# Attention, two-expert routing and an ELU layer on one core: rooms of 312 rows, a third conversion buffer with later stores, and ELU as a maximum

## The chip, the cores and the metric

The kernel is one program for one core of a Trainium2 chip. The metric is device time in microseconds (us). Five engines of the core matter here: TensorE (PE in the rows; its weight loads are PEld), VectorE (DVE), ScalarE (ACT), GpSimd (POOL) and SyncE (SP), which issues nearly all transfers (DMAs) and executes them strictly in its own order.

## What is computed

Three stages follow one another. Attention over 2 batches and 8 heads gives a matrix x of 1152 tokens by 512. A layer of 8 experts follows, of which each token uses two. A dense layer with an ELU ends the program. The reference, cut to the parts that the change touches:

```python
# experts: every token goes to the two experts with the largest noisy logits
for e in range(8):
    for k in range(2):
        mask = top2[:, k] == e
        h = np.maximum(x[mask] @ w1[e], 0.0)              # w1[e]: 512 x 1024
        out[mask] += top2_w[mask, k, None] * (h @ w2[e])  # w2[e]: 1024 x 512
# dense layer, w_in 512 x 2048 and w_out 2048 x 512, both float64
h = x @ w_in
g = np.where(h > 0.0, h, np.exp(np.minimum(h, 0.0)) - 1.0)
return g @ w_out
```

Counted with the reference on its own inputs, the eight experts receive 293, 306, 271, 255, 298, 284, 290 and 307 rows, and expert 0 receives 156 from the first batch and 137 from the second.

## The kernel before

**Rooms.** Each expert's rows are scattered into a room of fixed size in a DRAM tensor `xs`. Experts 1 to 7 have rooms of `CAP` = 336 rows; expert 0 has two rooms of `HC` = 168 rows, one per batch, together `E0` = 336. Rows beyond a room would be handled by a fallback (`overflow`), entered only if a count on the device is above zero. A whole room is computed, filled or not.

**Products.** Every float32 matrix product is made of three products of split operands (high and low halves in the `fp32r` type). ScalarE writes the high half, VectorE or GpSimd subtract it to get the low half. For an expert, layer 1 (L731) is 8 groups of 12 matmuls whose moving operand is a row block of `CAP` columns; layer 2 (`l2t`, L741) is 4 groups of 24 matmuls with `CAP` columns. Expert 0 has its own first layer (`First.l1`, L844, 168 columns), and expert 7 has a layer 2 in another form (`l2`, L759, 512 columns), in which the room's rows are the stationary operand.

**Conversions.** `w_in` and `w_out` arrive as float64. While the experts run, 32 pieces of them are converted with bit operations (`plan_convert`): a load of 512 KB into one of two `raw64` buffers (L697), four VectorE steps (L701 to L704), two GpSimd steps in place on the tile `cvm` (L707, L708), and a store of 256 KB to a DRAM tensor `wf` (L710), from which the dense layer later loads its weights.

**Order.** The order of work on all engines is written out: each step is given a time on an imaginary line (`ln.at`), and steps are emitted in the order of these times. An expert takes D = 29.7 units of the line; the conversion i stands at 16.5 + 5.99 i, its load 3 units before, its GpSimd steps 2 units behind, its store 6 units behind:

```python
m=s['m']=cv.tile([128,512],FT,name="cvm",bufs=2)
ln.at(t-3,load); ln.at(t,bits); ln.at(t+2,small); ln.at(t+6,store)
```

The time line sets only the order. When an instruction starts is decided by its engine's queue and by semaphores, so an instruction that waits holds up all that stand behind it on its engine. On SP a store that waits for GpSimd holds back the loads behind it.

**ELU.** The dense layer runs in three chunks of 384 tokens. For each of 16 groups of a chunk, PE makes `a` in PSUM (L972, 12 matmuls of 384 columns), `act` turns it into the halves g2h and g2l, and two groups later PE uses them in 9 matmuls of 512 columns (`outs`, L991). `act` has six steps, alternating between the engines:

```python
nc.scalar.activation(r,a[:,0:384],AF.Relu)
nc.vector.tensor_scalar(m,a[:,0:384],0.0,None,op0=OP.min)
nc.scalar.activation(m,m,AF.Exp)
nc.vector.scalar_tensor_tensor(r,m,-1.0,r,op0=OP.add,op1=OP.add)
```

then g2h on ScalarE (L981) and g2l on VectorE (L982). In the first chunk ScalarE and GpSimd also split the last weights (L670, L674).

## Time and profile before

| | before |
|---|---|
| median of the runs | 825.7 us (825.38, 825.7, 841.67) |
| profiled execution, its own time | 819.85 us |
| its span | 818.1 us, granted TensorE clock 0.99 of full speed |
| PE busy | 786.0 us, 96% |
| VectorE / ScalarE / GpSimd busy | 585.6 / 482.4 / 328.2 us |
| data moved | 119.82 MB, mean 146 GB/s |

The profile shows one execution, with times from the start of its span. The stages are read best by stretches: attention and the first layer of expert 0 up to about 336 us, the experts from there to about 607 us, the dense layer behind it. A busy PE is not a PE at its peak, since matmuls overlap; what a matmul costs is read from the distance between the starts of two matmuls in a row.

### The profile page before, as it was taken

To read this page: it belongs to the slowest core of one execution; us is meant where nothing else is said; L and a number is where in the kernel's file an instruction comes from. 1 tells how busy PE (TensorE), PEld (TensorE's weight loads), DVE (VectorE), ACT (ScalarE), POOL (GpSimd) and SP (SyncE) were. 2 spreads that over 40 slices of the span, in tenths; PEclk is the share of its full clock that TensorE was granted. 3 is DMA by queue.
4 is the path that set the end of the run, shared out by engine and by line. 5 is a ranking of instruction groups with operands and counts; after the bars stand their busy time and mean duration, and the time that the engine had idled before them with its cause. 6 is when DMAs were issued, how large, how long until landed. Compare 5 with 4: busy or idle time off the path is not lost.

```text
span 818.1 us, 13530 instructions
## 1 busy us (share of the span) xinstructions
PE 786.0 (96%) x4891; PEld 721.4 (88%) x4891; DVE 585.6 (72%) x1182; ACT 482.4 (59%) x1109; POOL 328.2 (40%) x303
## 2 busy tenths in 40 slices
PE   7999999999999999989999999999999899999997
PEld 5898989998888889979899999999887799999996
DVE  6888898898999876586968778687555644454443
ACT  5988888989888864434444445445345434334432
POOL 4634051431510765266666677666516602000000
PEclk8999999999999999989999999999999999999999
DMA  8029465131002245559688898986743203001001
GB/s 251 2 93 274 136 230 178 40 128 57 29 30 105 91 138 198 187 179 309 228 287 262 274 306 279 295 275 218 263 125 115 64 14 104 1 14 38 1 1 40
DMA packets 50984, 119.82 MB, mean 146 GB/s; under 512 B 7574, under 2 KB 8598, under 8 KB 50914
## 3 DMA queue, kind: packets, MB, share of 16 engines
q1 hardware_dynamic: 47922, 109.35, 40.6%
q0 software_dynamic: 2912, 9.44, 3.6%
q8 instruction: 40, 0.66, 0.3%
q14 instruction: 30, 0.25, 0.1%
q10 hardware_dynamic: 80, 0.13, 0.0%
HBM read 82.89 MB, written 36.01 MB: 145 GB/s over the span
## 4 chain that ended last, share of the span: by engine, by line
PE 30%; DMA 11%; DVE 9%; ACT 3%; issue 2%; POOL 2%; SPq 0%; DVEq 0%; POOLq 0%; ACTq 0%
PE o L991 11%; PE a L972 10%; PE oe L741 5%; DMA raw<-in_moe_w_in_dram 5%; DMA raw<-in_moe_w_dram 3%; PE ae L731 3%; DVE wl L674 2%; DMA raw<-in_moe_w_out_dram 2%; ACT wh L670 1%; DVE cvt L703 1%; DVE cvm L701 1%; DVE r L979 1%; DMA raw<-wf 1%; POOL cvm L708 1%; DVE cvt L704 1%
## 5 line engine op out<-in xcount | busy, mean ns | idle before, releaser
L293 ACT ACTIVATE p<-sp,m 128x384 f32<-128x384 f32 x216 | 125.1, 585 | 13.2 <-DVE m L285 13.0
L282 DVE TENSOR_REDUCE m<-sp 128x1 f32<-128x384 f32 x216 | 115.4, 550 | 20.6 <-PE sp L277 18.8
L674 POOL TENSOR_TENSOR wl<-raw,wh 128x1024 fp32r<-128x1024 f32 x32 | 80.8, 2530 | 59.3 <-ACT wh L670 59.2
L670 ACT ACTIVATE wh<-raw 128x1024 fp32r<-128x1024 f32 x76 | 79.8, 1057 | 37.9 <-DMA raw<-in_moe_w_dram 36.7
L305 DVE TENSOR_TENSOR pl<-t_p,ph 128x512 fp32r<-128x512 f32 x144 | 96.8, 683 | 6.0 <-ACT ph L302 4.2
L302 ACT ACTIVATE ph<-t_p 128x512 fp32r<-128x512 f32 x144 | 86.2, 603 | 16.7 <-PE t_p L299 11.3
L299 PE MATMUL t_p<-ident,p 128*128 128x128 f32 x576 | 83.3, 274 | 1.2 <-ACT xt L363 0.7
L277 PE MATMUL sp<-khl,qh 128*128 128x384 f32 x192 | 75.6, 394 | 4.2 <-ACT p L293 3.7
L299 PEld LDWEIGHTS t_p<-ident,p 128*128 128x128 f32 x576 | 67.9, 140 | 9.9 <-ACT xt L363 0.9
L707 POOL TENSOR_SCALAR cvm<-cvm 128x512 f32<-128x512 f32 x32 | 51.3, 1602 | 38.9 <-DVE cvm L701 38.9
L277 PE MATMUL sp<-khl,ql 128*128 128x384 f32 x192 | 65.7, 342 | 0.0
L674 DVE TENSOR_TENSOR wl<-raw,wh 128x1024 fp32r<-128x1024 f32 x44 | 63.4, 1453 | 2.6 <-ACT wh L670 2.6
L310 PE MATMUL o<-ph,vhl 128*128 128x512 f32 x144 | 63.8, 443 | 0.0
L991 PE MATMUL o<-wh,g2h 128*128 128x512 f32 x144 | 57.1, 396 | 3.9 <-ACT g2h L981 3.9
L234 POOL TENSOR_SCALAR kr<-kraw 128x576 fp32r<-128x576 f32 x14 | 9.5, 678 | 126.2 <-PE t_k L241 126.2
L311 PE MATMUL o<-pl,vhl 128*128 128x512 f32 x144 | 57.3, 398 | 1.0 <-DVE pl L305 1.0
L991 PE MATMUL o<-wh,g2l 128*128 128x512 f32 x144 | 56.8, 394 | 0.0
L991 PE MATMUL o<-wl,g2h 128*128 128x512 f32 x144 | 56.3, 391 | 0.0
L977 DVE TENSOR_SCALAR m<-a 128x384 f32<-128x384 f32 x48 | 26.7, 556 | 40.9 <-ACT r L976 40.2
L708 POOL TENSOR_TENSOR cvm<-cvm,cvt 128x512 f32<-128x512 f32 x32 | 48.0, 1501 | 17.3 <-DVE cvt L704 17.3
L979 DVE SCALAR_TENSOR_TENSOR r<-m,r 128x384 f32<-128x384 f32 x48 | 34.3, 714 | 28.4 <-ACT m L978 27.8
L701 DVE TENSOR_SCALAR cvm<-raw 128x512 int32<-128x512 int32 x32 | 26.9, 839 | 34.8 <-DMA raw<-in_moe_w_in_dram 19.9
(269 smaller groups left out, 1987.4 us busy)
## 6 DMA issues: line engine op xcount, KB each, us to landing
raw<-in_moe_w_dram SPq DMA_DIRECT2D x60, 512.0 KB, 7.1
raw<-in_moe_w_in_dram SPq DMA_DIRECT2D x16, 512.0 KB, 7.7
wf<-cvm SPq DMA_DIRECT2D x32, 256.0 KB, 2.8
raw<-in_moe_w_out_dram SPq DMA_DIRECT2D x16, 512.0 KB, 8.3
raw<-wf SPq DMA_DIRECT2D x16, 512.0 KB, 4.6
xs<-zrow SPq DMA_DIRECT2D x3, 1792.0 KB, 15.1
xs<-zrow SPq DMA_DIRECT2D x2, 2560.0 KB, 22.9
xe<-xs SPq DMA_DIRECT2D x7, 672.0 KB, 9.4
```

What stands on the lines that cost most here:

```text
L277: nc.tensor.matmul(sp[:,g,0:384],w,kh[:,h,384*(g0+g):384*(g0+g)+384],start=i==0,stop=i==len(ops)-1)
L282: nc.vector.tensor_reduce(m[:,x:x+1],s['s',j,x][:,:,0:384],axis=AX.XY,op=OP.max,negate=True)
L293: nc.scalar.activation(s['p',j][:,384*g0:384*(g0+nb)].rearrange("p (g n) -> p g n",g=nb),s.pop(('s',j,x))[:,:,0:384],AF.Exp,bias=m[:,3:4], ...
L299: nc.tensor.transpose(t[:,jj*128:jj*128+128],s['p',4*h+jj][:,kt*128:kt*128+128],ident)
L302: nc.scalar.activation(ph,s['tp',h,kt],AF.Copy)
L305: nc.vector.tensor_tensor(pl,s.pop(('tp',h,kt)),s['ph',h,kt].bitcast(FT),op=OP.subtract)
L310: nc.tensor.matmul(s['o',h],w,s.pop(('ph',h,kt)),start=kt==0,stop=False)
L311: nc.tensor.matmul(s['o',h],w,s.pop(('pl',h,kt)),start=False,stop=kt==8)
L670: s.tc.nc.scalar.activation(w[0][:,p['i']*p['n']:(p['i']+1)*p['n']],p['r'],AF.Copy)
L674: e.tensor_tensor(w[1][:,sl],p['r'],w[0][:,sl].bitcast(FT),op=OP.subtract)
L972: nc.tensor.matmul(a[:,0:384],wv[:,c,fs],xv[:,c],start=n==0,stop=n==11); n+=1
L991: nc.tensor.matmul(O[i],gv[:,ts],wv[:,f%8],start=f==0 and n==0,stop=f==15 and n==2)
```

## The change

Three edits. The rooms of experts 1 to 7 shrink to 312 rows, and expert 0 keeps its 336. The conversions follow one another every 5.7 units of the line (5.99 before), their stores stand 8 units behind (6 before), and `cvm` has three buffers (two before). In `act` the first step becomes Relu(-a) on ScalarE, the exponential is taken of its negative on ScalarE, and one VectorE step makes max(exp - 1, a), reading `a` from PSUM; the step L977 goes away. Since 104 rows (a third of a room) and 84 rows are no multiples of 16, loads and stores of rooms are issued in two strips (96 and 8 rows, 80 and 4 rows). The diff, cut to what has a part in the time:

```diff
+def strips(m):
+    return [(a,b) for a,b in ((0,m//16*16),(m//16*16,m)) if b>a]
-HC=168; E0=2*HC; CAP=336; C3=CAP//3; OVR=102; OV0=E0+7*CAP; OVN=1632; NROW=OV0+OVN+128; NDUMP=20*128
+HC=168; E0=2*HC; CAP=312; C3=CAP//3; EM=max(E0,CAP); OVR=105; OV0=E0+7*CAP; OVN=1680; NROW=OV0+112*17; NDUMP=20*128
...
-        f=s['f']=cv.tile([128,512],I32,name="cvt",bufs=2); m=s['m']=cv.tile([128,512],FT,name="cvm",bufs=2)
+        f=s['f']=cv.tile([128,512],I32,name="cvt",bufs=2); m=s['m']=cv.tile([128,512],FT,name="cvm",bufs=3)
...
-    ln.at(t-3,load); ln.at(t,bits); ln.at(t+2,small); ln.at(t+6,store)
+    ln.at(t-3,load); ln.at(t,bits); ln.at(t+2,small); ln.at(t+8,store)
...
-        nc.sync.dma_start(s['x'],ap(xs,(E0+e*CAP-CAP)*512,[[1536,C3],[512,3],[1,512]]))
+        for a,b in strips(C3): nc.sync.dma_start(s['x'][a:b],ap(xs,(E0+e*CAP-CAP+3*a)*512,[[1536,b-a],[512,3],[1,512]]))
...
-    nc=tc.nc; s={}
+    nc=tc.nc; s={}; R=E0 if first else CAP
...
-                nc.tensor.matmul(o[:,0:CAP],wv[:,f,cs],hv[:,f],start=n==0,stop=n==23); n+=1
+                nc.tensor.matmul(o[:,0:R],wv[:,f,cs],hv[:,f],start=n==0,stop=n==23); n+=1
...
-        nc.scalar.activation(r,a[:,0:384],AF.Relu)
-        nc.vector.tensor_scalar(m,a[:,0:384],0.0,None,op0=OP.min)
-        nc.scalar.activation(m,m,AF.Exp)
-        nc.vector.scalar_tensor_tensor(r,m,-1.0,r,op0=OP.add,op1=OP.add)
+        nc.scalar.activation(m,a[:,0:384],AF.Relu,scale=-1.0)
+        nc.scalar.activation(m,m,AF.Exp,scale=-1.0)
+        nc.vector.scalar_tensor_tensor(r,m,-1.0,a[:,0:384],op0=OP.add,op1=OP.max)
...
-OVF=True; T0=20; TG=4.32; WARM=8; MW=((0,2,3),(12,14,3),'pppp','pppp'); CNT=(13.2,13.9); CV=(16.5,5.99)
+OVF=True; T0=20; TG=4.32; WARM=8; MW=((0,2,3),(12,14,3),'pppp','pppp'); CNT=(13.2,13.9); CV=(16.5,5.7)
```

The order on three engines shows where the edits move work. On SP, in the stretch of experts 2 and 3, before: `wf` is a conversion's store, `raw_NNNN` its load, plain `raw` a piece of an expert's weights.

```order
L710 DMA wf_64<-cvm 128x512
L668 DMA raw<-in_moe_w_dram 128x2x512
L697 DMA raw_5960<-in_moe_w_in_dram 128x1024
L668 DMA raw<-in_moe_w_dram 128x2x512
L710 DMA wf_64<-cvm 128x512
L668 DMA raw<-in_moe_w_dram 128x2x512
L697 DMA raw_6020<-in_moe_w_in_dram 128x1024
```

The same place now (lines are four higher in the changed file):

```order
L714 DMA wf_64<-cvm 128x512
L701 DMA raw_5938<-in_moe_w_in_dram 128x1024
L672 DMA raw<-in_moe_w_dram 128x2x512
L714 DMA wf_64<-cvm 128x512
L672 DMA raw<-in_moe_w_dram 128x2x512
L701 DMA raw_5983<-in_moe_w_in_dram 128x1024
L672 DMA raw<-in_moe_w_dram 128x2x512
L714 DMA wf_64<-cvm 128x512
L701 DMA raw_6065<-in_moe_w_in_dram 128x1024
```

At two of these three places the conversion's load has moved up to stand right behind a store, where a piece of weights stood between; the piece of weights now stands ahead of the store. No load has come to stand ahead of the store two conversions back.

On VectorE, in the first layer of expert 1, before: `hl` are the low halves that layer 2 uses, `wl` those of weights, `cvm` and `cvt` the four steps of a conversion.

```order
L733 SCALAR_TENSOR_TENSOR hl<-ae,hh 128x336 x3
L674 TENSOR_TENSOR wl<-raw,wh 128x1024
L733 SCALAR_TENSOR_TENSOR hl<-ae,hh 128x336
L701 TENSOR_SCALAR cvm<-raw_5411 128x512
L702 TENSOR_SCALAR cvt<-raw_5411 128x512
L703 SCALAR_TENSOR_TENSOR cvt<-raw_5411,cvt 128x512
L704 SCALAR_TENSOR_TENSOR cvt<-raw_5411,cvt 128x512
L733 SCALAR_TENSOR_TENSOR hl<-ae,hh 128x336 x2
```

And now:

```order
L737 SCALAR_TENSOR_TENSOR hl<-ae,hh 128x312 x3
L678 TENSOR_TENSOR wl<-raw,wh 128x1024
L705 TENSOR_SCALAR cvm<-raw_5395 128x512
L706 TENSOR_SCALAR cvt<-raw_5395 128x512
L707 SCALAR_TENSOR_TENSOR cvt<-raw_5395,cvt 128x512
L708 SCALAR_TENSOR_TENSOR cvt<-raw_5395,cvt 128x512
L737 SCALAR_TENSOR_TENSOR hl<-ae,hh 128x312 x3
L678 TENSOR_TENSOR wl<-raw,wh 128x1024
L737 SCALAR_TENSOR_TENSOR hl<-ae,hh 128x312
L705 TENSOR_SCALAR cvm<-raw_5506 128x512
L706 TENSOR_SCALAR cvt<-raw_5506 128x512
```

A second conversion now falls among the eight `hl` steps of this layer, where there was one.

On ScalarE, two groups at the start of the dense layer, before and now: `wh` are high halves of weights.

```order
L976 ACTIVATE r_8020<-a_8007 128x384
L978 ACTIVATE m_8021<-m_8021 128x384
L981 ACTIVATE g2h<-r_8020 128x384
L670 ACTIVATE wh<-raw 128x1024 x2
```

```order
L980 ACTIVATE m_8037<-a_8023 128x384
L981 ACTIVATE m_8037<-m_8037 128x384
L984 ACTIVATE g2h<-r_8036 128x384
L674 ACTIVATE wh<-raw 128x1024 x2
```

ScalarE keeps its four kinds of steps in the same order; the second now reads what the first wrote, with no VectorE step between them.

## Rows read from the trace of the kernel before

**Rows 1.** Busy us by stretch: PE, PEld, DVE, ACT, POOL; clock, DMA share, GB/s.
```profile
336.00:565.00 229.00, 217.88 (x1410) 212.69 (x1411) 175.54 (x241) 106.79 (x179) 150.28 (x84) 0.98 0.82 270
...
607.00:640.00 33.00, 29.07 (x144) 25.11 (x144) 17.43 (x21) 16.67 (x28) 17.06 (x8) 1.00 0.39 128
640.00:818.10 178.10, 173.54 (x887) 157.10 (x885) 82.69 (x149) 69.59 (x139) 14.25 (x13) 1.00 0.11 32
```

**Rows 2.** Timeline of PE, expert 6 and 7 begin layer 1: start, us, instruction.
```profile
530.91 0.77 PE L731 MATMUL ae<-xh,wh 128*128 128x336 f32 x4
...
564.76 0.78 PE L731 MATMUL ae<-xh,wh 128*128 128x336 f32 x4
```

**Rows 3.** Timeline of PE in waits of layer 2 and transposes: idle before, releaser.
```profile
351.53 1.38 PE L722 MATMUL te<-ident,xe 112*128 112x112 f32 x6 [3.44 <-DVE xl L724]
...
390.55 0.73 PE L722 MATMUL te<-ident,xe 112*128 112x112 f32 x4 [1.66 <-DVE xl L724]
...
515.85 0.42 PE L741 MATMUL oe<-hh,wh 128*128 128x336 f32 x1 [0.83 <-ACT hh L732]
```

**Rows 4.** Groups of PE by form: line, form, count; busy, mean ns; idle before.
```profile
L731 PE MATMUL ae<-xh,wh 128*128 128x336 f32 x224 | 44.9, 322 | 2.4 <-DVE hl L733 2.4
L741 PE MATMUL oe<-hh,wh 128*128 128x336 f32 x224 | 43.5, 336 | 2.9 <-ACT hh L732 2.5 <-PEq L555 0.4
L991 PE MATMUL o<-wh,g2h 128*128 128x512 f32 x144 | 57.1, 396 | 3.9 <-ACT g2h L981 3.9
```

**Rows 5.** Timeline of PE, 168 columns (58 starts apart) and 336 (52 apart).
```profile
329.05 0.28 PE L844 MATMUL a<-x1h,w0l 128*128 128x168 f32 x1
...
335.53 0.27 PE L844 MATMUL a<-x1l,w0h 128*128 128x168 f32 x1
...
472.46 0.77 PE L731 MATMUL ae<-xh,wl 128*128 128x336 f32 x4
...
480.43 0.77 PE L731 MATMUL ae<-xl,wh 128*128 128x336 f32 x4
```

**Rows 6.** Timeline of PE, 12 of 384 columns, then 9 of 512.
```profile
700.47 0.86 PE L972 MATMUL a<-x2h,wh 128*128 128x384 f32 x4
...
702.55 0.39 PE L991 MATMUL o<-wh,g2h 128*128 128x512 f32 x1
...
704.60 0.86 PE L972 MATMUL a<-x2h,wh 128*128 128x384 f32 x4
```

**Rows 7.** Timeline of DVE at the dense layer's start, and POOL beside it.
```profile
618.57 0.56 DVE L977 TENSOR_SCALAR m<-a 128x384 f32<-128x384 f32 x1 [1.72 <-ACT r L976]
619.72 2.73 DVE L979 SCALAR_TENSOR_TENSOR r<-m,r 128x384 f32<-128x384 f32 x1 [0.59 <-ACT m L978]
...
617.29 4.74 POOL L674 TENSOR_TENSOR wl<-raw,wh 128x1024 fp32r<-128x1024 f32 x2 [2.00 <-ACT wh L670]
```

**Rows 8.** Timeline of PE there: start, us, idle before and its releaser.
```profile
620.48 0.86 PE L972 MATMUL a<-x2l,wh 128*128 128x384 f32 x4
623.05 0.50 PE L991 MATMUL o<-wh,g2h 128*128 128x512 f32 x1 [1.72 <-ACT g2h L981]
```

**Rows 9.** Two VectorE lines: count, ns min/median/max, first and last start.
```profile
L979 DVE SCALAR_TENSOR_TENSOR r<-m,r x48: 557/558/2728, 610.7 to 809.2; 128x384 f32<-128x384 f32 x48
...
L733 DVE SCALAR_TENSOR_TENSOR hl<-ae,hh x56: 493/501/510, 363.8 to 581.5; 128x336 fp32r<-128x336 f32 x56
```

**Rows 10.** Chain of waits through one pair of conversions: start, us, what.
```profile
476.03 8.45 DMA raw<-in_moe_w_out_dram
...
489.41 0.33 SPq L710
...
490.31 4.67 DMA raw<-in_moe_w_out_dram
```

**Rows 11.** Who waited for whom: us in total, times, longest.
```profile
SPq L710 <- POOL cvm L708: 129.6, 30, 8.8
...
DVE cvm L701 <- DMA raw<-in_moe_w_in_dram: 19.9, 8, 4.8
```

More of the change, by code (lines that the diff above doesn't have):

```diff
@@ L431, in fill @@
         return f
-    return [fill(xs,OV0+OVN,80,32,a,a+16) for a in (0,16)]+[fill(xs,0,OV0//24,24,a,a+8) for a in range(0,24,8)]+[fill(ys,OV0-CAP,C3,3,0,3)]+[fill(ys,OV0,110,16,a,a+4) for a in range(0,16,4)]
+    return [fill(xs,OV0+OVN,80,32,a,a+16) for a in (0,16)]+[fill(xs,0,112,24,a,a+8) for a in range(0,24,8)]+[fill(ys,OV0-CAP,112,3,0,3)]+[fill(ys,OV0,112,17,a,min(a+5,17)) for a in range(0,17,5)]
 def gating(tc, g, grp, b, tiles, cp, wk, psf, X, L, xs, scat):
@@ L556, in overflow @@
         with tc.tile_pool(name="ov",bufs=1) as op_:
-            nc.sync.dma_start(ap(xs,OV0*512,[[16*512,110],[512,16],[1,512]]),g['z'][0:110,None,:].to_broadcast([110,16,512]))
+            nc.sync.dma_start(ap(xs,OV0*512,[[15*512,112],[512,15],[1,512]]),g['z'][:,None,:].to_broadcast([112,15,512]))
             ov=g['ov']; ob=op_.tile([128,8],FT,name="ovb0")
@@ L725, in l1 @@
     def l1(f):
-        if f==0: s['hh']=hp.tile([128,8,CAP],FR,name="hh"); s['hl']=hp.tile([128,8,CAP],FR,name="hl")
+        if f==0: s['hh']=hp.tile([128,8,EM],FR,name="hh")[:,:,0:CAP]; s['hl']=hp.tile([128,8,EM],FR,name="hl")[:,:,0:CAP]
         wh,wl=wt[0]['w']; hh,hl=s['hh'],s['hl']
@@ L734, in l2t @@
     def l2t(c):
-        if c==0: s['yt']=xp.tile([128,4,CAP],FT,name="yt",bufs=1)
+        if c==0: s['yt']=xp.tile([128,4,EM],FT,name="yt",bufs=1)
         wh,wl=wt[1]['w']; hh,hl=first or (s['hh'],s['hl'])
@@ L740, in l2t @@
             for f in range(8):
-                nc.tensor.matmul(o[:,0:CAP],wv[:,f,cs],hv[:,f],start=n==0,stop=n==23); n+=1
+                nc.tensor.matmul(o[:,0:R],wv[:,f,cs],hv[:,f],start=n==0,stop=n==23); n+=1
     def evt(c):
-        nc.scalar.activation(s['yt'][:,c],s['o',c][:,0:CAP],AF.Copy)
+        nc.scalar.activation(s['yt'][:,c,0:R],s['o',c][:,0:R],AF.Copy)
     def tr(j):
         h,r,m=(j//2,j%2,HC//2) if first else (0,j,C3)
-        if r==0: s['y',h]=xp.tile([m,CAP//m if not first else 2,512],FT,tag="ye",name="ye",bufs=1)
+        if r==0: s['y',h]=xp.tile([m,2 if first else 3,512],FT,tag="ye",name="ye",bufs=1)
         t=ps.tile([128,512],FT,tag="t",name="ty",bufs=2)
@@ L750, in store0 @@
     def store0(h):
-        nc.sync.dma_start(ap(ys,h*HC*512,[[1024,HC//2],[512,2],[1,512]]),s['y',h])
+        for a,b in strips(HC//2): nc.sync.dma_start(ap(ys,(h*HC+2*a)*512,[[1024,b-a],[512,2],[1,512]]),s['y',h][a:b])
     def l2(j):
@@ L769, in store @@
     def store():
-        nc.sync.dma_start(ap(ys,(E0+e*CAP-CAP)*512,[[1536,C3],[512,3],[1,512]]),s['y',0])
+        for a,b in strips(C3): nc.sync.dma_start(ap(ys,(E0+e*CAP-CAP+3*a)*512,[[1536,b-a],[512,3],[1,512]]),s['y',0][a:b])
     if not first:
@@ L812, in load @@
     def load(s):
-        s.tc.nc.sync.dma_start(s.xe,ap(s.xs,0,[[1024,HC//2],[512,2],[1,512]]))
+        for a,b in strips(HC//2): s.tc.nc.sync.dma_start(s.xe[a:b],ap(s.xs,a*1024,[[1024,b-a],[512,2],[1,512]]))
     def xt(s, psf, i):
@@ L846, in relu @@
         nc=s.tc.nc
-        if b==0 and f==0: s.h=[hp.tile([128,8,CAP],FR,tag=f"h{x}",name=f"h{x}") for x in "hl"]
+        if b==0 and f==0: s.h=[hp.tile([128,8,EM],FR,tag=f"h{x}",name=f"h{x}") for x in "hl"]
         v=a[:,0:n*HC].rearrange("p (f n) -> p f n",f=n)
@@ L906, in gather @@
     def gather(i, k):
-        if (i,k)==(0,0): s['y1']=xp.tile([128,4,CAP],FT,tag="yt",name="yl1",bufs=1).rearrange("p a b -> p (a b)")
+        if (i,k)==(0,0): s['y1']=xp.tile([128,4,EM],FT,tag="yt",name="yl1",bufs=1).rearrange("p a b -> p (a b)")
         if k==0: Y[i]=[lp.tile([128,512],FT,name="yl0",bufs=3),s['y1'][:,i%2*512:i%2*512+512]]
```

## Prediction

> **What bounds the kernel now.** I read the stretches first, to see which stage an edit can reach, then the distance between matmuls, since a busy PE says little of what a column costs, then the waits of PE, and last the chain of waits through the conversions. In the expert stretch PE is busy 217.88 of 229 us, VectorE 175.54, and the DMA engines 0.82 of the time; in the bulk of the dense layer PE is busy 173.54 of 178.1 us, and at its start 29.07 of 33 [rows 1]. So PE is the first bound everywhere, and the experts stand close to a second one: an expert takes 33.85 us from one first layer to the next [rows 2], and what idle time PE has there comes from VectorE or ScalarE being late: 3.44, 1.66 and 0.83 us are the largest of it [rows 3]. The granted clock is 0.98 there, 1.00 behind it [rows 1].
>
> What is late behind VectorE is shown by the chain through a pair of conversions. A conversion's load takes 8.45 us, its store is issued 4.93 us after the load landed (489.41 less 484.48), and the load of the next conversion but one, which needs the same buffer, is issued at 490.31, right behind that store on SP: a cycle of 14.28 us for two conversions [rows 10]. SP stood 129.6 us in 30 waits at such stores, 4.3 us each, and VectorE 19.9 us in 8 waits for the loads of `w_in` alone [rows 11]. On the line two conversions take 2 x 5.99 = 11.98 units; at 33.85 us for 29.7 units that is 13.65 us. The cycle and the PE time of an expert thus lie near each other.
>
> **Smaller rooms.** The matmuls that lose 24 columns are, by the counts of the groups, 3 x 224 = 672 of layer 1 and 3 x 224 - 96 = 576 of layer 2, since expert 0 keeps 336 and expert 7's layer 2 streams 512 columns either way [rows 4]. That is 1248. What a column costs: matmuls of 168 columns start every 6.48 us / 58 = 111.7 ns, of 336 every 7.97 / 52 = 153.3 ns [rows 5], of 384 every 2.08 / 12 = 173.3 ns and of 512 every 2.05 / 9 = 227.8 ns [rows 6]. Between 336 and 384 a column costs 0.417 ns, between 384 and 512 0.426; between 168 and 336 only 0.248, so there is a floor somewhere below. If the upper line goes on, it meets the 111.7 ns at about 237 columns, and 312 lies well above. I take 10.0 ns for 24 columns, 12.5 us for all; the lower bound is the flat slope, 5.9 ns and 7.4 us. The 84 transposes at the input lose 8 of 112 columns, 3.3 ns each by the same slope: 0.3 us.
>
> The Trainium skill, in "TensorE: Matmul & The Clock Gate", section "Back-to-back issue gap", speaks against this: it gives about 81 ns per matmul at 128 columns and 131 ns at 512 for streams in which each matmul has its weight load, which is 0.13 ns a column and would make the term 3.9 us, an estimate. This trace does not agree: 227.8 ns at 512 columns, with a weight load each.
>
> The steps of VectorE and ScalarE on the rooms shorten by 24 columns too, but beside PE. The strips add 17 issues on SP of about 0.33 us each, as the store's issue shows [rows 10]; 6 us, covered by the 129.6 us that SP waits anyway [rows 11]. If that cover went, each would delay the loads behind it by 0.33 us.
>
> **Conversions.** The number of steps stays 32 each; their places move. By the order on SP the load of a conversion now mostly stands right behind the store two conversions earlier, where a 512 KB piece of weights stood between, and weights that stood behind a store now stand ahead of it. Nothing moves ahead of the store that gates the load, so the cycle remains: load, VectorE, GpSimd, store, load. Its need gets tighter. With the columns gone an expert should take about 33.85 - 1.9 = 31.9 us, and two conversions 2 x 5.7 / 29.7 of it, 12.25 us. Without the transfer the cycle is 14.28 - 8.45 = 5.83 us, so the transfer must land within 6.4 us. Loads land between 4.67 and 8.45 us after their issue in the two rows that I show [rows 10]. With less put ahead of them, and the third `cvm` buffer removing the wait for an earlier store to land, I expect the lower half of that: 4.67 gives a cycle of 10.5 us. Then the waits of 1.66 and 0.83 us [rows 3], both behind work that SP had released late, should mostly go: up to 11.1 us of idle time in the stretch less the 3.44 us that comes ahead of the first conversion's end, so at most 7.7 us. Against it, a second conversion now falls among the `hl` steps of a layer 1, from which PE's `a` buffers come free; PE waited 2.4 us for `hl` in that group so far [rows 4]. If each of seven experts gets one more wait like the 0.83 us, 5.8 us are lost. From +5.8 to -7.7 I take -1.0: gains and losses of the same size, with a small lean to the side on which the loads move. The DMA share would go from 0.82 to about 0.87 when the stretch shrinks by 12 us, below what would stop it by itself.
>
> **ELU.** PE's idle time for g2h is 3.9 us in all [rows 4]; one of its pieces, 1.72 us, is shown [rows 8], the other is 2.2. The cause: the step L979 took 2.73 us and ended at 622.45, 0.42 us after GpSimd's two weight steps had ended at 622.03 [rows 7]. It has both inputs in SBUF and needs 558 ns alone; L733, of the same kind with one input in PSUM, never took over 510 ns though GpSimd works in that stretch too [rows 9]. The new step reads `a` from PSUM, so it should not wait. It also starts 0.6 us sooner, because L977 with its 0.56 us stands no longer between the two ScalarE steps [rows 7].
>
> The Trainium skill, "SBUF — State Buffer", section "SBUF: two separate sides", has the rule: a VectorE instruction with two SBUF inputs and a GpSimd instruction that reads SBUF exclude each other for the whole instruction. By that rule the wait moves on to g2l, which still has two SBUF inputs; the trace agrees as far as L979 goes.
>
> In times: the new step runs from about 619.1 to 619.7, g2h is there by 620.3, g2l has to stand until 622.03 and ends at 622.45. PE comes free of L972 at 621.34 [rows 8], has two products of 0.23 us that need g2h alone, and waits 0.7 us for g2l, where it waited 1.72. With the other piece shortened as much, 2.1 us are gained; at most 3.9, at least nothing, if g2l were held longer. The 48 instructions of L977 that go cost nothing elsewhere, since PE does not wait for them in the bulk of the layer. That `a` is held until VectorE has read it is hidden: a group takes PE 4.13 us [rows 6] and there are three buffers.
>
> **Sum.** 12.5 + 0.3 + 1.0 + 2.1 = 15.9 us off. The profiled execution took 819.85 us, so 804.0; the median of the runs is 5.85 us higher, and the same step gives **809.8 us**, 1.9% less.
>
> **Rivals.** (a) *The conversions set the pace, and the kernel gets slower.* If their loads go on landing in 8.45 us, 16 cycles of 14.28 us are 228 us, all of the stretch as now, and the experts cannot use their shorter matmuls. But the last conversion stands 31 x 0.29 = 9 units earlier on the line, so 9 units of expert work, 9.7 us at 31.9 us for 29.7, come behind it where they lay beside it. Less 1 us of columns behind that point and 2.1 of ELU: +6.6, 832 us. It decides from a cycle of 12.25 us. For it: the cycle as read. Against: its transfer is the part that the new order relieves. 7%.
> (b) *VectorE's order gives half back.* PE with shorter groups waits for `hl` and `xl` behind the denser conversions; 6.4 of 12.8 us return, no ELU loss: 816 us. VectorE is busy 77% of the stretch, and much of the rest is waiting in order. 18%.
> (c) *Columns cost less than I say*, the flat slope of the rows: 7.4 in place of 12.5: 815 us. 7%.
> (d) *All waits fall*: 12.8 + 7.7 + 3.9 = 24.4: 801 us; parts of it up to 806. 15%.
> (e) *The change does not do what it says*, because a room overflows and the fallback runs: the fullest room gets 307 rows of 312, so below 1%.
> The forecast, 805 to 815 us, has 50%; 2% or so is for what I have not thought of.
>
> About 2% is what a measurement of this kernel can tell from no change: that is below 809.2 us or above 842. Below it lie (d) and a little over half of the forecast's own spread, 42%; above 842 only the tail of (a), 2%. The range is 802 to 820 us; it leaves out (a), the ends of (b) and (d), and the unknown, less than 2 in 10.
>
> **What would show it.** Starts of L731 and L741 at 143 ns; an expert of 31 to 32 us; if 148 ns, (c). Loads of conversions that land in 5 to 6 us with cycles near 12 us, and the last one earlier against its expert; if cycles stay near 14 us and PE's idle time in the stretch grows, (a). More PE idle time for `hl` or `xl`, above 15 us in the stretch, would be (b). At the dense layer's start, the maximum step at 0.6 us throughout, g2l at up to 2 us, and PE idle 1 to 2 us in place of 3.9. I am wrong if attention or the bulk of the dense layer changes by over a microsecond.

## The result and the profile after

The changed kernel takes 818.0 us (median of 12 runs, 808.12 to 841.07); the kernel before, beside it, 825.54 us (12 runs, 815.79 to 841.67). The ratio is **0.9888, 95% interval 0.9846 to 0.993**: 1.1% faster, where the forecast said 1.9%. Both kernels spread over 25 us and more between runs; where a profile caught it, most of that was a drop of the TensorE clock ahead of the experts, in code that the change does not touch (last section), so ratios come from undisturbed runs, and profiles are compared from expert 0's layer 2 on.

The profiled execution, the fastest of the 12, took 808.12 us, its span 806.3. PE was busy for 768.7 us of it (95%; before 786.0), VectorE 560.9 (585.6), ScalarE 481.0 (482.4), GpSimd 332.4 (328.2).

The stretches of after: expert 0's layer 2 (334.3 to 357.1, 22.8 us, PE busy 18.73); then six expert periods, from expert 1's first layer 1 to expert 7's; then to the dense layer's first matmul; then the rest. The last three as rows, columns as in [rows 1].

```profile
357.10:559.10 202.00, 186.44 (x1302) 181.42 (x1301) 163.73 (x225) 95.07 (x163) 144.79 (x81) 0.99 0.85 283
559.10:600.00 40.90, 40.75 (x240) 35.65 (x238) 22.47 (x45) 18.33 (x31) 12.99 (x9) 1.00 0.42 141
600.00:806.30 206.30, 201.76 (x1033) 183.26 (x1032) 74.18 (x122) 87.82 (x168) 31.67 (x20) 1.00 0.15 48
```

The last three of these stretches in the kernel before (the first is 336.2 to 358.5, 22.3 us, with PE busy 18.85):

```profile
358.50:564.80 206.30, 198.84 (x1302) 193.91 (x1302) 158.97 (x223) 96.65 (x163) 135.99 (x78) 0.99 0.84 275
564.80:606.40 41.60, 41.51 (x239) 37.02 (x238) 24.95 (x47) 18.66 (x31) 17.30 (x13) 1.00 0.48 166
606.40:818.10 211.70, 203.21 (x1033) 182.53 (x1031) 100.72 (x170) 86.83 (x168) 31.31 (x20) 1.00 0.15 47
```

From expert 0's layer 2 to the end it is 481.9 us before and 472.0 after, 9.9 us less: +0.5, -4.3, -0.7 and -5.4 by stretch. In the six periods PE's busy time fell by 12.40 us, as the columns should make it, but the time by 4.3 only: PE now idles 15.56 us of them (202.00 less 186.44), before 7.46. An expert takes 33.7 us (202.0 / 6), before 34.4, and not the 31 to 32 us forecast. The dense layer gave 5.4 us, more than twice its forecast.

Groups of PE in after, as in [rows 4]:

```profile
L994 PE MATMUL o<-wh,g2h 128*128 128x512 f32 x144 | 56.7, 394 | 0.0
L735 PE MATMUL ae<-xh,wh 128*128 128x312 f32 x224 | 42.9, 314 | 5.4 <-DVE hl L737 5.4
...
L745 PE MATMUL oe<-hh,wh 128*128 128x312 f32 x192 | 33.4, 314 | 4.8 <-ACT hh L736 4.8
...
L745 PE MATMUL oe<-hl,wh 128*128 128x312 f32 x192 | 32.3, 309 | 3.2 <-DVE hl L737 3.2
L726 PE MATMUL te<-ident,xe 104*128 104x104 f32 x84 | 10.8, 265 | 5.9 <-DVE xl L728 5.9
```

The dense layer's 3.9 us of waiting for g2h are gone. Layer 1 waits 5.4 us for `hl` (2.4 before), and layer 2 waits for `hl` too, 3.2 us, which it did not before. Transposes wait 5.9 us for `xl` (5.8 before), and layer 2 4.8 us for `hh` from ScalarE (2.5 before). How such a wait comes about is seen at expert 1. First VectorE:

```profile
367.13 1.22 DVE L678 TENSOR_TENSOR wl<-raw,wh 128x1024 fp32r<-128x1024 f32 x1
368.27 0.42 DVE L705 TENSOR_SCALAR cvm<-raw 128x512 int32<-128x512 int32 x1
368.60 0.42 DVE L706 TENSOR_SCALAR cvt<-raw 128x512 int32<-128x512 int32 x1
369.06 0.98 DVE L707 SCALAR_TENSOR_TENSOR cvt<-raw,cvt 128x512 int32<-128x512 int32 x1
...
370.68 0.87 DVE L737 SCALAR_TENSOR_TENSOR hl<-ae,hh 128x312 fp32r<-128x312 f32 x2
...
377.09 0.43 DVE L705 TENSOR_SCALAR cvm<-raw 128x512 int32<-128x512 int32 x1 [1.07 <-DMA raw<-in_moe_w_in_dram]
...
379.52 0.47 DVE L737 SCALAR_TENSOR_TENSOR hl<-ae,hh 128x312 fp32r<-128x312 f32 x1
```

and PE beside it:

```profile
371.21 0.84 PE L735 MATMUL ae<-xh,wh 128*128 128x312 f32 x4 [1.35 <-DVE hl L737]
...
380.05 0.42 PE L745 MATMUL oe<-hl,wh 128*128 128x312 f32 x1 [1.32 <-DVE hl L737]
```

One `wl` and one conversion occupy VectorE from 367.13 to 370.68; the `hl` behind them frees PE's buffer at 371.2, and PE has stood 1.35 us. Then a conversion waits 1.07 us for its load, at the head of VectorE's queue, while the last `hl` of the layer stands behind it: PE stands another 1.32 us. It is the layer whose order on VectorE stands in the section on the change. In the kernel before it had one such wait, where a conversion alone stood in front of the `hl`:

```profile
375.12 0.89 PE L731 MATMUL ae<-xh,wh 128*128 128x336 f32 x4 [1.27 <-DVE hl L733]
```

### The profile page after: what moved, and what is told of

Same layout as the page of the kernel before. It is cut to its first block, busy times and chain, and to the rows that moved or that the text cites. A ratio compares the mean times of both kernels' runs of the same rounds, so it can differ in the third digit from the quotient of the medians.

```text
span 806.3 us, 13467 instructions
## 1 busy us (share of the span) xinstructions
PE 768.7 (95%) x4891; PEld 706.1 (88%) x4891; DVE 560.9 (70%) x1134; ACT 481.0 (60%) x1109; POOL 332.4 (41%) x303
## 4 chain that ended last, share of the span: by engine, by line
PE 32%; DMA 11%; DVE 9%; issue 2%; POOL 2%; ACT 1%; SPq 1%; DVEq 0%; POOLq 0%; ACTq 0%
PE a L976 12%; PE o L994 12%; DMA raw<-in_moe_w_in_dram 4%; PE oe L745 4%; DMA raw<-in_moe_w_out_dram 3%; DVE wl L678 2%; DVE cvt L707 2%; PE ae L735 2%; DMA raw<-in_moe_w_dram 2%; DVE cvm L705 2%; DVE cvt L706 1%; POOL cvm L712 1%; DMA raw<-wf 1%; PE ac L926 1%; DVE cvt L708 1%
## 5 line engine op out<-in xcount | busy, mean ns | idle before, releaser
L678 POOL TENSOR_TENSOR wl<-raw,wh 128x1024 fp32r<-128x1024 f32 x32 | 84.2, 2640 | 30.8 <-ACT wh L674 29.5
L982 DVE SCALAR_TENSOR_TENSOR r<-m,a 128x384 f32<-128x384 f32 x48 | 26.6, 554 | 86.7 <-ACT m L981 86.6
L678 DVE TENSOR_TENSOR wl<-raw,wh 128x1024 fp32r<-128x1024 f32 x44 | 66.5, 1521 | 2.6 <-ACT wh L674 2.6
L980 ACT ACTIVATE m<-a 128x384 f32<-128x384 f32 x48 | 23.4, 488 | 64.3 <-PE a L976 64.3
L712 POOL TENSOR_TENSOR cvm<-cvm,cvt 128x512 f32<-128x512 f32 x32 | 50.2, 1568 | 17.7 <-DVE cvt L708 17.1
L985 DVE TENSOR_TENSOR g2l<-r,g2h 128x384 fp32r<-128x384 f32 x48 | 33.4, 696 | 28.4 <-ACT g2h L984 28.4
```

The lines of the kernel that those rows point to most:

```text
L678: e.tensor_tensor(w[1][:,sl],p['r'],w[0][:,sl].bitcast(FT),op=OP.subtract)
L712: nc.gpsimd.tensor_tensor(m,m,s['f'].bitcast(FT),op=OP.mult)
```

## Experiments

Times of a stretch are from one profile of each kernel. "Six" are the six expert periods as above, "idle" is their length less PE's busy time; "VectorE" and "ScalarE" are PE's waits in them for `hl` and `xl`, and for `hh`; "last" is from expert 7's layer 1 to the dense layer. All in us; the clock is that granted in the six periods.

| kernel | six | idle | VectorE | ScalarE | clock | last | dense | ratio to before |
|---|---|---|---|---|---|---|---|---|
| before | 206.3 | 7.5 | 4.7 | 2.5 | 0.99 | 41.6 | 211.7 | 1 |
| after | 202.0 | 15.6 | 10.4 | 4.8 | 0.99 | 40.9 | 206.3 | 0.9888 |
| rooms_only | 202.5 | 12.6 | 10.8 | 1.1 | 0.99 | 46.0 | 212.8 | 1.0051 |
| conv_only | 205.5 | 9.0 | 4.6 | 4.2 | 1.00 | 41.6 | 211.8 | 1.0124 |
| elu_only | 205.6 | 7.5 | 6.2 | 1.1 | 1.00 | 41.6 | 206.1 | 0.9913 |
| no_conv_edit | 198.0 | 10.7 | 8.9 | 1.2 | 1.00 | 45.6 | 206.0 | 0.9939 |
| store_behind | 199.5 | 11.5 | 7.0 | 4.1 | 0.98 | 40.8 | 206.1 | 0.9894 |
| pool_short | 201.1 | 13.9 | 5.0 | 8.7 | 0.97 | 40.9 | 206.1 | one run |
| vector_short | 199.5 | 12.1 | 2.4 | 9.4 | 0.97 | 40.9 | 206.2 | one run |
| both_short | 193.1 | 9.4 | 0.7 | 8.4 | 0.99 | 40.8 | 206.0 | one run |
| no_conversions | 187.3 | 5.3 | 0 | 5.0 | 1.00 | 40.8 | 206.2 | one run |
| last_on_vector | 212.6 | 19.9 | 16.9 | 2.7 | 0.95 | 40.8 | 206.0 | 1.0141 |
| shifted_work | 232.6 | 32.7 | 28.8 | 3.7 | 0.92 | 41.1 | 206.0 | 1.0347 |
| shifted_early | 228.8 | 31.2 | 26.6 | 4.4 | 0.93 | 41.3 | 206.0 | 1.0349 |

How far one profile can be trusted is seen in the table itself: the three kernels with rooms of 336 rows have six periods of 205.5 to 206.3 us, but rooms_only and no_conv_edit differ by 4.5 us, though they have the same experts and conversions. So a difference of 4.5 us in "six" decides nothing by itself. The smaller rooms stand out in all that have them: with the whole work of the conversions, six periods take 198.0 to 202.5 us and idle 10.7 to 15.6 in the four kernels of 312 rows (after, rooms_only, no_conv_edit, store_behind), 205.5 to 206.3 and 7.5 to 9.0 in the three of 336.

### One part alone, and all but one

**rooms_only** takes the edits of `CAP` and the strips from the change and leaves conversions and `act` as before; **elu_only** takes `act` alone; **conv_only** the conversions alone; **no_conv_edit** is the change with the conversions as before:

```diff
-    ln.at(t-3,load); ln.at(t,bits); ln.at(t+2,small); ln.at(t+8,store)
+    ln.at(t-3,load); ln.at(t,bits); ln.at(t+2,small); ln.at(t+6,store)
-CV=(16.5,5.7)
+CV=(16.5,5.99)
```

(and `cvm` back to two buffers).

> Smaller rooms alone: conversions spaced 5.99, store 6 behind, two cvm buffers, the old ELU. Theory A (the cycle of a conversion's load, VectorE, GpSimd, store and next load sets the experts' pace): the experts' stretch, 228.6 us from the first L741 to expert 7's first layer before, stays within 3 us of that, PE idle time in it grows from 10.9 to about 20 us, and the whole is 1 to 4 us faster than before. Theory B (PE sets the pace and the denser conversions of the change took the gain back): the stretch shrinks by 9 to 12 us with idle time near 11 us, and the whole is 10 to 13 us faster than before. Matmuls of L735 start 143 ns apart in both.

> The ELU edit alone on the kernel before. Both theories: the experts' stretch stays at 228 to 229 us; at the dense layer's start the 3.9 us of PE idle time go, so 4 to 5 us faster than before. By the step of the prediction that moved the wait on to g2l it would be 2.1 us.

> The change without its edit of the conversions (5.99 apart, store 6 behind, two buffers). If the edit only takes from what smaller rooms give: 2 to 8 us faster than the changed kernel. If smaller rooms give nothing without it, as the run of the rooms alone says: 1.005 of before for the rooms and 0.991 for ELU, so about 0.996 of before, 6 us slower than the changed kernel, with conversions that reach into expert 7 (store of the last one later than 565 us).

> The kernel before with only the conversions' edit (5.7 units apart, three cvm buffers, stores 8 units behind). If its gain is that the last conversions leave expert 7, as the kernel with the two other edits suggests (45.6 us from expert 7's first layer to the dense layer, 40.9 with this edit), then with rooms of 336 rows, where that distance was 41.6 us already, it gives nothing: 822 to 828 us, ratio 0.997 to 1.003, and the experts' stretch stays at 225 to 229 us. If denser conversions cost by themselves, the stretch grows to 232 us or more and the time is above 829. If they feed the chain better, the stretch falls below 222 and the time below 819.

Measured: rooms_only 1.0051 (0.9995 to 1.0108), elu_only 0.9913 (0.9857 to 0.9968), no_conv_edit 0.9939 (0.9891 to 0.9987), conv_only 1.0124 (1.0006 to 1.0242).

Smaller rooms alone gain nothing, and rooms_only fits neither expectation: its stretch from expert 0's layer 2 to expert 7 is 225.3 us, 3.3 less than before. Its experts are faster by about what after's are, 3.8 us of the six periods, but behind them 4.4 us come back. The last conversions come late there. In rooms_only the last store of a conversion stands here on SP, 5.0 us behind the start of expert 7's layer 1 (560.8):

```profile
565.83 0.32 SPq L714 DMA_DIRECT2D wf<-cvm  x1
```

and PE waits twice in that stretch, by the waits of rooms_only:

```profile
PE ac L926 <- DVE ysp L770: 2.0, 1, 2.0
PE ae L735 <- DVE hl L737: 1.5, 1, 1.5
```

Behind the one for `ysp`, which ends at 599.80, PE also runs at a lower clock to the end of the stretch (columns as in [rows 1]):

```profile
599.80:606.80 7.00, 7.00 (x31) 7.00 (x32) 2.99 (x5) 1.79 (x4) 0.00 (x0) 0.76 0.43 127
```

Together, PE idles 3.5 us of the 46.0, in after 0.15 of 40.9, and is busy 1.7 us longer. In after the last store is at 552.52, 6.6 us ahead of expert 7 (559.10):

```profile
337.44 0.45 SPq L701 DMA_DIRECT2D raw<-in_moe_w_in_dram  x1
...
552.52 0.34 SPq L714 DMA_DIRECT2D wf<-cvm  x1
```

no_conv_edit shows the same as rooms_only there, 45.6 us. So the conversions' edit is worth 4.7 us in that stretch, and only where the rooms are small: with rooms of 336 rows the stretch is 41.6 us with it and without it. That it is worth as much in the whole time is not shown: the six periods are 198.0 us without it and 202.0 with it, and the intervals of no_conv_edit and after overlap. In the kernel before, the last store also came 3.9 us behind expert 7's start, at no cost. One thing that differs at 5.0 us is the wait for the converted weights that are loaded back from `wf`. ScalarE in this stretch of rooms_only:

```profile
ACT wh L674 <- DMA raw<-wf: 4.1, 1, 4.1
```

It is 3.9 us in no_conv_edit, and 0.8 in before and in after. That this wait passes through VectorE to PE's two is read from the traces; no run tried it. A VectorE step of expert 7's output (L915, 0.48 us in its other places) also falls beside a GpSimd subtraction there and takes 2.65 and 2.62 us in rooms_only and no_conv_edit, 0.85 in after. conv_only's ratio above 1 is not explained by its experts, which took the usual time; its profile had the low clock ahead of them, and with four runs the interval only just leaves out 1. From expert 0's layer 2 to the end its profile takes 481.2 us, before 481.9. I take it as no gain; a loss of 1% is not ruled out.

Of the whole, then, the ELU edit alone gives 0.9913 and all three edits 0.9888, with intervals that overlap. That rooms and conversions together add to ELU is seen in the stretches of single profiles (4.5 us), not in the ratios.

### Which part of a conversion holds the experts

**no_conversions** leaves the 32 conversions out and loads expert weights for the dense layer. **vector_short** leaves out three of the four VectorE steps, **pool_short** replaces the two GpSimd steps by a copy of 16 columns, **both_short** does both, so that little more than the transfers is left:

```diff
-        V.tensor_scalar(f,hi,3,0x3FFFFFF8,op0=OP.logical_shift_left,op1=OP.bitwise_and)
-        V.scalar_tensor_tensor(f,hi,-0x40000000,f,op0=OP.bitwise_and,op1=OP.bitwise_or)
-        V.scalar_tensor_tensor(f,lo,29,f,op0=OP.logical_shift_right,op1=OP.bitwise_or)
...
-        nc.gpsimd.tensor_scalar(m,m,2.0**-15*1.125,None,op0=OP.is_ge)
-        nc.gpsimd.tensor_tensor(m,m,s['f'].bitcast(FT),op=OP.mult)
+        nc.gpsimd.tensor_copy(m[:,0:16],m[:,16:32])
```

> Left out: the 32 conversions; the dense layer's weights are loaded from expert weights of the same size instead. What PE alone would do: by theories A and C an expert falls to about 31 us, PE idle time in the stretch to 6 us or less (4 of it before the second expert), the stretch to about 211 us and the whole to 790 to 795 us in its profiled execution. If the stretch stays above 220 us, it is not the conversions that take the gain.

> The changed kernel without three of the four VectorE steps of each conversion (the float32 words are not put together, so the dense layer's weights are wrong); transfers and both GpSimd steps stay. The stretch is 224.8 us in the changed kernel and 203.2 without conversions. Theory C1 (VectorE's own work, some 2 us per conversion, in its order): stretch 205 to 211 us. Theory C2 (GpSimd's steps hold VectorE and the store): 215 to 223. Theory D (the conversions' transfers crowd out those of weights): 220 to 225.

> The changed kernel with the two GpSimd steps of each conversion replaced by a copy of 16 columns (the words are stored unfinished); transfers and the VectorE steps stay. C1: stretch 217 to 224 us. C2: 205 to 212 us, VectorE's longest conversion steps back to 0.35 us. D: 220 to 225 us.

> The changed kernel with one VectorE step and a GpSimd copy of 16 columns for each conversion (the words are wrong); only the transfers stay as they are. C1 and C2: stretch 203 to 207 us, near that without conversions. D: 215 to 225 us, with ScalarE's waits for weights (34 us in the changed kernel) as long or longer.

Measured, one run each: 787.42, 802.04, 814.91 and 819.22 us, of which only the stretches of the table can be compared, since pool_short and both_short had the low clock ahead of the experts. Without conversions six periods take 187.3 us, so the conversions cost the changed kernel 14.7 us there. Most of it, 8.9 us, goes when VectorE's and GpSimd's steps go and the transfers stay; 5.8 us stay with the transfers and the step that is left. From expert 0's layer 2 to expert 7, the stretch of the expectations, vector_short takes 219.3 us and pool_short 223.0, so neither C1 nor C2 holds alone; both_short takes 211.3, between what C1 and C2 wanted and D; no_conversions takes 203.2, where 211 was expected. Who is waited for changes with it. The longest sum of PE's waits in the six periods of vector_short and no_conversions (8.4 us of the same kind in both_short):

```profile
PE oe L742 <- ACT hh L733: 9.4, 6, 3.4
```

```profile
PE oe L745 <- ACT hh L736: 5.0, 5, 1.7
```

The waits for VectorE fall from 10.4 us to 2.4, 0.7 and nothing as its steps go. In their place layer 2 waits for the last `hh` from ScalarE, which stands in order behind the high halves of weights; ScalarE waited 34.0 us for those pieces to land in after, 45.6 in vector_short, 40.1 in pool_short, 40.9 in both_short and 24.7 in no_conversions. This fits that one cause taken away alone gives little (0.9 us in pool_short, 2.5 in vector_short, both within the spread): behind VectorE's order stands that of ScalarE and the transfers. With one profile each, it is a reading and not a proof.

### The wait of SP at the stores

**store_behind** puts the store 9 units behind the conversion in place of 8, so that the load two conversions later stands ahead of it on SP:

```diff
-    ln.at(t-3,load); ln.at(t,bits); ln.at(t+2,small); ln.at(t+8,store)
+    ln.at(t-3,load); ln.at(t,bits); ln.at(t+2,small); ln.at(t+9,store)
```

> The changed kernel with each conversion's store one unit later (9 in place of 8), so that on SP the load of the next conversion but one stands ahead of it and no longer waits for GpSimd. Theory A: loads are issued 1.5 to 4 us earlier against their conversion, VectorE's waits for them (29 us in the changed kernel) fall below 15 us, PE idle time in the stretch falls from 19.6 to 10 to 14 us, the whole is 5 to 9 us below the changed kernel. Theory C (VectorE, working in its own order and held by GpSimd's steps, sets the pace): the waits for loads fall, but PE idle time stays above 17 us and the whole is within 2 us of the changed kernel.

Measured: 0.9894 (0.9845 to 0.9944), the same as after. SP's waits in the six periods, after and then store_behind:

```profile
SPq L714 <- POOL cvm L712: 101.3, 23, 8.0
```

```profile
SPq L701 <- DVE cvt L708: 47.9, 17, 4.6
SPq L714 <- POOL cvm L712: 31.1, 19, 6.1
```

101.3 us of waiting at stores fell to 31.1, but the load ahead of the store now waits 47.9 us for its buffer, which VectorE frees. The gate moved from GpSimd and the store to VectorE, and the time did not follow. So SP's wait for GpSimd at the stores, on which the prediction spent most words, is not what costs the experts their gain. The run does not free the conversions as a whole: from the first load to the last store they took 215.6 us, in after 215.1, and VectorE waited 24.0 us for their loads, in after 29.2. Of what was expected, the time is that of theory C; PE's idle time in the stretch, 15.9 us (after 19.6), lies between the two.

### VectorE's order, tried the other way

**last_on_vector** computes the two GpSimd steps as one on VectorE, right behind the other four. **shifted_work** also gives GpSimd three of four subtractions of the experts' weights, where it had one or two. **shifted_early** is shifted_work with the stores 4 units behind:

```diff
-        nc.gpsimd.tensor_scalar(m,m,2.0**-15*1.125,None,op0=OP.is_ge)
-        nc.gpsimd.tensor_tensor(m,m,s['f'].bitcast(FT),op=OP.mult)
+        V.scalar_tensor_tensor(m,m,2.0**-15*1.125,s['f'].bitcast(FT),op0=OP.is_ge,op1=OP.mult)
...
-WP['2'][2],'vpvv'
+WP['2'][2],'vppp'
```

> After, with the two GpSimd steps of a conversion (1.60 and 1.57 us) made one VectorE step, (m >= c) * f, right behind the other four; it computes the same. The chain loses GpSimd: by the theory that the conversions' chain sets the experts' pace, the store is ready some 3 us or more sooner, SP waits less, and GpSimd no longer shares SBUF with VectorE for 101 us: stretch 216 to 221 us in place of 224.8, time 808 to 814. The rival, that VectorE's own order is the limit: 32 steps of about 0.6 to 0.9 us more on VectorE, 18 to 28 us busy, of which the experts feel a part: stretch 226 to 232, time 818 to 826.

> As last_on_vector, and GpSimd takes the subtractions of three of four pieces of the experts' weights (one or two of four in after). VectorE loses about as much as it got, GpSimd's 101 us are filled with about 24 subtractions of 2.67 us, 64 us. If VectorE's order is a limit, this is faster than last_on_vector by 3 to 6 us: stretch 212 to 217, time 804 to 811. If weights that come later (2.67 us in place of about 1.1) hold PE, it is slower than last_on_vector, 2 to 8 us.

> As shifted_work, with the store 4 units behind the conversion in place of 8: it now waits for VectorE alone, which has done its five steps in 3 to 4 us, so SP stands less at stores and the load two conversions on is no longer issued right behind the wait. If SP's wait at stores paces the loads: 2 to 4 us faster than shifted_work, SP's waits at stores below 40 us. If the transfers themselves do (DMA share 0.88 and more), no difference within 1.5 us.

Measured: 1.0141 (1.0049 to 1.0233), 1.0347 (1.0223 to 1.047) and 1.0349 (1.0219 to 1.0479). The first is what VectorE's order predicts, and more: the six periods take 10.6 us longer, PE's waits for VectorE rise from 10.4 to 16.9, and the clock falls to 0.95 behind them. (Its profile also has the low clock ahead of the experts, which the six periods leave out.) VectorE's busy time rose by only 8.2 us (171.97 against 163.73), since some of its steps got shorter without GpSimd's beside them (`wl` 1.33 us in the mean, in after 1.56). Whether it is the longer block in front of an `xl` or `hl` that counts, or VectorE's load, the run does not separate: both grew.

The second missed both expectations: it should have gained by relieving VectorE, or lost 2 to 8 us, and its six periods took 20.0 us more than last_on_vector's. Of these, 12.8 us are idle time of PE, 11.9 of it in waits for VectorE; the rest, 7.2 us, is busy time of PE, at a clock of 0.92 in place of 0.95. One place, VectorE first, then GpSimd and PE:

```profile
432.91 1.84 DVE L705 TENSOR_SCALAR cvm<-raw 128x512 int32<-128x512 int32 x1
434.67 2.62 DVE L706 TENSOR_SCALAR cvt<-raw 128x512 int32<-128x512 int32 x1
437.33 2.75 DVE L707 SCALAR_TENSOR_TENSOR cvt<-raw,cvt 128x512 int32<-128x512 int32 x1
...
441.45 0.86 DVE L727 TENSOR_TENSOR xl<-te,xh 128x312 fp32r<-128x312 f32 x2
...
431.69 7.84 POOL L678 TENSOR_TENSOR wl<-raw,wh 128x1024 fp32r<-128x1024 f32 x3 [6.17 <-ACT wh L674]
...
441.98 0.80 PE L734 MATMUL ae<-xl,wh 128*128 128x312 f32 x2 [3.03 <-DVE xl L727]
```

Three subtractions in a row on GpSimd run to 439.53, and three of the five VectorE steps take 1.84, 2.62 and 2.75 us beside them, against 0.42, 0.42 and 0.98 at 368.27 in after. The conversion holds VectorE for 8.5 us, and PE waits 3.03 us for the `xl` behind it. Work that was taken off VectorE's queue came back as longer steps in it: in the six periods its subtractions of weights took 25.1 us less than in last_on_vector, and the five steps of the conversions 24.0 us more. The rival, that low halves of weights come later and hold PE, finds no support: none of PE's waits, and none of its weight loads', names them. shifted_early has the same ratio: where the stores stand made no difference here either.

No kernel tried beats after; store_behind equals it, and the intervals of elu_only and no_conv_edit overlap with its own.

## Why the prediction was right, and where it was not

The time lies inside the range, and less than 2% was the likelier outcome by the chances given; the forecast's own 805 to 815 us, which had 50%, missed it. The forecast of 1.9% was too good by 0.8 points, by two errors of opposite sign. The experts' waits cost 9.8 us more than the sum had, and ELU gave 3.3 us more; that the second took back a third of the first is luck.

**Columns: right.** Matmuls of 312 columns start 143.5 ns apart (20 of them from 468.19 to 471.06; see the last section's rows), 9.8 ns less than the 153.3 of 336; the sum took 10.0. PE's busy time from expert 0's layer 2 to the dense layer fell by 13.3 us (259.20 to 245.92), where 12.8 was the term.

**The step that failed: "From +5.8 to -7.7 I take -1.0".** The waits of the experts were to shrink a little and grew by more than the bound: rooms and conversions together took 4.5 us off (+0.5, -4.3, -0.7) where PE's own work lost 13.3, so +8.8 in place of -1.0. The bound was one more wait like the 0.83 us of [rows 3] per expert. In fact the waits became longer and hardly more: in the six periods PE waited 13 times for `hl`, `xl` and `hh`, 15.2 us in all, before 12 times, 7.2 us. The price of a wait was taken from a row of the old kernel; but a layer 1 group takes PE 1.72 us now (12 x 143.5 ns), before 1.84 (12 x 153.3), while a `wl` and a conversion in front of an `hl` take VectorE as long as before (1.22 and 2.5 us at expert 1 in both kernels, where nothing holds them up). What PE had gained on each group became a wait where it used to be slack. That is rival (b), "VectorE's order gives half back", which had 18%; its sign, more than 15 us of idle time for `hl` or `xl`, was missed by a little (5.9, 5.4 and 3.2, 14.5 us, before 8.2; with 4.8 for ScalarE and the rest, PE idles 19.8 us in the three stretches ahead of the dense layer, before 11.0). Of the two causes that (b) named together, shorter groups and denser conversions, the runs lay most to the first: the waits for VectorE in the six periods are 7.0 to 10.8 us in the four kernels of 312 rows (10.8 and 8.9 with the old conversions, in rooms_only and no_conv_edit), and 4.6 to 6.2 in the three of 336 (4.6 with the new conversions, in conv_only). What the denser conversions bring is a kind of wait: layer 2 waits for `hl` 2.5 to 3.2 us in after, store_behind, pool_short and conv_only, and never in before, rooms_only, elu_only and no_conv_edit, and it waits 4.1 us or more for `hh` in the first four of these, 2.5 or less in the last four.

**Conversions' cycle: the reading was right, its weight wrong.** From the first load to the last store the 32 conversions took 215.1 us, before 230.2 (338.55 to 568.74): over 16 that is 13.4 us for two, before 14.4. They followed the line, as forecast, but 13.4 is nearer to the 14 us of rival (a) than to the 12 that were to show the forecast, and their loads did not land in "the lower half" of 4.67 to 8.45 us. Nine loads stand in after's chain of waits, of 3.69 to 10.26 us; four landed within 6.5, five took longer. Two of them:

```profile
400.76 6.35 DMA raw<-in_moe_w_in_dram
...
412.82 7.51 DMA raw<-in_moe_w_in_dram
```

Rival (a), the cycle as the pace and a slower kernel, did not come: the kernel is faster, and store_behind took SP's wait out of the cycle without an effect on the time. What the edit did bring, that the last conversions leave expert 7, stood in rival (a) as "come behind it" and had no term in the sum; it is worth 4.7 us in its stretch and cancels the same loss of the smaller rooms.

**ELU: mechanism right, size wrong.** The sum had 2.1 us, at most 3.9; elu_only and after show 5.6 and 5.4. Two things were mis-sized. First, the ceiling: the 3.9 us are PE's idle time, and a wait can also lie in the weight loads while matmuls are still in the pipe. From one profile to the other, PE's idle time in the dense layer fell by 3.95 us (8.49 to 4.54), and its busy time by 1.45 (203.21 to 201.76), with the same matmuls: together 5.4. Who waited for g2l in the kernel before (us, times):

```profile
  PEld o L991: 1.5, 5
```

These five waits of 0.3 us, 1.5 us in all, beside which matmuls took up to 0.50 us in place of 0.39, are gone in after, as are five of PEld for g2h, 5.1 us, which hold the 3.9. That the 1.5 us are the 1.45 of busy time is read from their size. Second, g2l did take the lock as forecast, and it cost nothing. VectorE and PE in after:

```profile
610.81 0.55 DVE L982 SCALAR_TENSOR_TENSOR r<-m,a 128x384 f32<-128x384 f32 x1 [2.05 <-ACT m L981]
611.96 2.21 DVE L985 TENSOR_TENSOR g2l<-r,g2h 128x384 fp32r<-128x384 f32 x1 [0.59 <-ACT g2h L984]
...
615.29 0.39 PE L994 MATMUL o<-wh,g2l 128*128 128x512 f32 x1
```

This g2l, held 2.21 us, ends at 614.17; PE wants it at 615.29. The forecast let the chain of this group start 0.6 us sooner than in the row of before, and it started 2.0 us sooner: ScalarE takes it up 9.75 us behind the dense layer's first matmul (609.75 less 600.0), before 11.72 (618.06 less 606.34). ScalarE in the kernel before, and then in after:

```profile
612.72 0.47 ACT L976 ACTIVATE r<-a 128x384 f32<-128x384 f32 x1
...
615.73 0.53 ACT L981 ACTIVATE g2h<-r 128x384 fp32r<-128x384 f32 x1 [1.39 <-DVE r L979]
616.16 1.99 ACT L670 ACTIVATE wh<-raw 128x1024 fp32r<-128x1024 f32 x2
618.06 0.47 ACT L976 ACTIVATE r<-a 128x384 f32<-128x384 f32 x1
```

```profile
605.78 0.47 ACT L980 ACTIVATE m<-a 128x384 f32<-128x384 f32 x1
...
609.75 0.47 ACT L980 ACTIVATE m<-a 128x384 f32<-128x384 f32 x1
```

Two causes add up. Each of the two groups ahead lost the VectorE step between ScalarE's first two, which brings every later group forward by 0.6 us: the group ahead starts 5.78 us behind the first matmul, before 6.38. And the long VectorE step of the group ahead (L979) had held ScalarE's g2h for 1.39 us in place of 0.62, and with it the two weight steps and this group's first step behind them: 0.77 us. I took the start of the chain from the old trace as given, though the same edit had brought it forward in the groups ahead.

The new step reads PSUM and stayed at 540 to 556 ns in all 48 cases, and g2l went from 559 ns throughout to a longest of 2365:

```profile
L982 DVE SCALAR_TENSOR_TENSOR r<-m,a x48: 540/554/556, 603.8 to 796.8; 128x384 f32<-128x384 f32 x48
```

```profile
L985 DVE TENSOR_TENSOR g2l<-r,g2h x48: 557/559/2365, 605.0 to 798.0; 128x384 fp32r<-128x384 f32 x48
```

The rule of the Trainium skill, "SBUF — State Buffer", section "SBUF: two separate sides", that VectorE and GpSimd share a port, agrees with both rows, and with the steps of 2.62 and 2.75 us in shifted_work. Of these, the one of 2.62 us (L706) reads only one tensor, so a VectorE step with a single input in SBUF can be held up too.

**Attention and the bulk of the dense layer.** The bulk did not change, as said: its last 177 us (from 640.96 before, from 629.28 now) are the same to 0.1 us, and groups follow one another every 4.13 us. Attention was 1.9 us shorter in the profile, more than the microsecond that was to show me wrong: expert 0's first layer begins at 304.22 us, before at 306.10. The edits need not be the cause: store_behind, with after's code there, begins it at 306.51, and in the first 60 us the clock was 1.00 in after and 0.94 in before.

## What to carry to other kernels

When PE's work in a stage shrinks, the work of the in-order engines beside it does not: compare the longest block on VectorE that can stand in front of a step that PE waits for (3.5 us at expert 1) with PE's time for as many groups as it has buffers, before counting the saved columns as time. A ceiling on what a wait can give back needs the waits of the weight loads beside PE's idle time, and a chain that is late is followed back to the first group in which its cause appears, not to the one with the longest wait. Moving work from VectorE to GpSimd did not free VectorE here, where both worked in SBUF; look at the durations of the steps beside it first. And a change of several edits is to be set beside its best single edit: here ELU alone came within the noise of all three.
